# A planned Nyström attention and SiLU layer: q, k, landmarks and exp(C) of the later batches turned by DMA, scores over 64 rows

## The chip, the cores and the metric

The kernel runs on one core of a Trainium2 chip. TensorE (PE) multiplies into PSUM, VectorE (DVE) and ScalarE (ACT) read PSUM and write SBUF, GpSimd (POOL) works on SBUF alone, and SyncE (SP) issues DMAs. POOL issues DMAs too. Each engine runs its own instructions in order and waits on semaphores for the others. The metric is the time of one execution in microseconds (us).

## What is computed

For 8 batches of 8 heads, with a sequence of 576 and a head of 64, the reference computes attention with 32 landmarks, which are means over 18 neighbouring rows, and then a layer with SiLU:

```python
q_lm = q.reshape(B, H, m, S // m, D).mean(axis=3)
k_lm = k.reshape(B, H, m, S // m, D).mean(axis=3)
A = sm(q, k_lm)
Bm = sm(q_lm, k_lm)
C = sm(q_lm, k)
Z = Bm.transpose(0, 1, 3, 2) / (norm1(Bm) * norminf(Bm) + 1e-06)
for _ in range(6):
    Z = 2 * Z - Z @ Bm @ Z
attn = A @ Z @ C @ v
h = x @ w_in                       # x: attn with the heads side by side
out = (h * (1.0 / (1.0 + np.exp(-h)))) @ w_out
```

`sm` is a softmax over products scaled by 1/8. All inputs and the output are float32; the kernel works in bfloat16 with float32 sums.

## The kernel before

**One batch.** The 8 heads of a batch are held as two groups (`qd`) of four. The rows of q and k (`qn`, `kn`) come from HBM with 128 pairs of head and landmark on the partitions and 18 rows of 64 in each. `landmarks` sums the 18 rows: on TensorE for batches 0 to 2, on POOL from batch 3 on (`tree`, then `lm`). `turn` (lines 459 and 466) and the end of `landmarks` (line 446) turn q, k and the landmarks on VectorE. Its turn works in blocks of 32 by 32 words of 32 bits, so that the 64 numbers of a head end up as 32 partitions with pairs side by side. A score over 64 numbers is therefore two products over 32 rows (`o` = 0 and 1), the second added to the first: `scores_b` for Bm, `scores_a_of` for A and `scores_c` for C. From batch 2 on, those of Bm and A are one block of 48 products.

After the scores, VectorE takes maxima (`cmax`, `bmax`, `amax`), ScalarE takes exponentials (`exps_c` writes `pc`, which is exp(C), `exps_a` writes `ea`), and `values` turns `pc` with 12 products by an identity matrix on TensorE into PSUM, copies the result to `pt` (line 711; on VectorE from batch 2 on) and multiplies it with v (`vn`): C v. `norm_b` and `steps_x` are a serial chain of small products on TensorE and copies on VectorE that gives Z C v, and `z_of` brings it into the form `zt`. `weights_a` normalizes `ea` and turns it into `at`.

**The two layers.** `mix` multiplies `zt` with `w_in` into `m`, in products of 64 rows by 512 columns (64*32). `layer1` multiplies `m` with `at` (rows `h<-at,m`), and ScalarE writes SiLU of it to `g`. `layer2` multiplies `g` with `w_out` (rows `o<-w_out_sb,g`, 512 columns, 16 products for a tile of 128 rows of the output), ScalarE copies it to one of four buffers `ost`, and SP stores it, 64 rows a DMA.

**Buffers.** `qT` and `kT` exist once; `qn`, `kn`, `vn`, `lm` and `lmT` twice, in turn. A load of q or k for batch b + 2 goes into the buffer that batch b's turns read. PSUM is held as two double banks `h`, two banks `o` and two banks `t`.

**The order.** Every operation is recorded in `_Plan` with an engine, a cost and a priority, with the buffers that it reads and writes. `SEQ` is the order in which the steps are recorded (E: one batch's attention, M: its mix, L: its layer 1 or a part of it), `SHIFT` changes single priorities, `XM` is a margin behind which `layer1`'s products are taken as ready. `schedule` gives each operation a start and puts each engine's instructions out in that order. The costs only choose the order: what runs on the chip is that order, with semaphores where the data demands them. Nearly all products are issued in one helper, line 243, and are told apart by their tiles.

Of the kernel before, what the change touches and what calls it, by code (L numbers as in the profile page):

```python
# [8 lines left out]
BF = mybir.dt.bfloat16  # L9
# [7 lines left out]
SEQ = ['E0', 'M0', 'S1', 'L0', 'X1', 'K2', 'M1', 'E2', 'L1', 'E3', 'M2', 'L2.0.4', 'L2.4.16', 'M3', 'E4', 'L3', 'M4', 'E5', 'L4', 'E6', 'M5', 'L5', 'E7', 'M6', 'L6', 'M7', 'L7']  # L17
# [3 lines left out]
SHIFT = {'DVE gx t 3': 2.5, 'DVE qT qn 3': -0.25, 'POOL ea arec 1': 1, 'DVE lmT lm 3': 3.0, 'PE t gx 3': 2, 'DVE crec csum 3': -0.25, 'DVE asum ea 0': -0.5, 'POOL kn 1': -0.5, 'DVE at ea 3': 2, 'DVE asum ea 2': 2.5, 'ACT ea s 3': 1.0, 'PE t qn 0': -1, 'DVE bs t 3': -0.5, 'POOL qn 3': -1, 'DVE m h 0': -1.75, 'POOL kn 3': -1.0, 'DVE qT qn 1': 1, 'POOL bmd bm 0': -0.25, 'POOL kn 2': -2.5, 'DVE pt h 1': 2, 'PE t gx 2': -1, 'PE t xp 0': -0.25, 'PE t lmT 1': 0, 'ACT ea s 1': 1, 'ACT xp h 0': -2, 'PE t bt 1': 2, 'DVE m o 0': 2, 'ACT lm h 2': 0.5, 'DVE bm t 3': 0.25, 'DVE m h 1': 1, 'PE t gc1g 0': 0.5, 'DVE cmax h 2': 0.25, 'PE h m 0': -2, 'DVE mask 0': 0.5, 'DVE bsum t 1': -0.25, 'PE o g 0': 0.5, 'DVE at ea 2': 0.5, 'PE o g 2': 2, 'DVE kT kn 0': -1, 'POOL bmd bm 2': -1, 'PE t lmT 2': 0.5, 'DVE n t 1': -2, 'PE t kn 0': 1, 'DVE at ea 0': 1, 'POOL vn 1': 2, 'PE h m 2': -0.25, 'PE o lmT 0': 1, 'PE h pt 1': -0.25, 'DVE rn n 2': 3, 'PE o g 1': 2, 'DVE gc0t t 1': 0.5, 'PE t lmT 3': -0.5, 'PE t bt 0': 0.25, 'ACT ost3b o 3': 0.25, 'PE h zt 0': 1, 'DVE lmT lm 2': -2, 'PE h zt 1': 1, 'DVE n t 2': 1, 'POOL qn 1': -0.5, 'DVE brec bsum 3': 0.5, 'DVE bt gc0t 1': 2, 'DVE brec bsum 1': 0.25, 'DVE cneg cmax 3': 1, 'ACT t bs 2': -1, 'DVE bmax t 2': -0.25, 'POOL bmd bm 3': -0.25, 'DVE gc0g t 1': -0.25, 'POOL ea arec 2': 2, 'POOL tree kn 3': 2, 'DVE lmT lm 1': -0.5, 'POOL qn 0': -0.25, 'DVE gc1g t 1': 0.25, 'DVE bs t 2': 0.5, 'DVE bsum t 3': 0.5, 'DVE n t 5': -0.25, 'PE t qn 1': 0.5, 'DVE bm t 7': -1, 'PE h pc 0': -0.25, 'PE t kn 1': -0.5, 'DVE s h 6': -2, 'DVE bmax t 7': -0.5, 'ACT pc h 6': 0.5, 'PE h lmT 3': -1, 'PE t bm 3': 0.25, 'DVE rn n 1': 0.25, 'DVE bt bm 2': 0.25, 'DVE amax s 7': -0.5, 'ACT pc h 1': -0.5, 'POOL qn 4': -0.5, 'DVE pt h 2': 0.25, 'DVE kT kn 2': -0.5, 'DVE pt h 4': 0.25, 'DVE n t 3': 1, 'DVE bmd t 0': -2, 'DVE bs t 1': 1, 'ACT m h 5': 1, 'DVE bmax t 1': -2, 'ACT ost o 7': 1, 'DVE crn crec 0': -0.5, 'PE t gc0t 1': 0.5, 'PE t xp 2': -1, 'PE t gx 5': 2, 'DVE gx t 2': 1, 'DVE kT kn 3': 0.25, 'PE o g 3': 2, 'DVE pt h 7': -1, 'DVE crec csum 7': -1, 'PE h zt 3': -1}  # L21
# [4 lines left out]
FLAGS = {'st0': 'DDDAAA', 'st1': 'DAAADD', 'pt0': 'SS', 'pt1': 'SA', 'sub0': 'DP', 'sub1': 'PD', 'mul0': 'PP', 'mul1': 'PP', 'lm1': 'EE', 'lm2': 'EE', 'lz': 1}  # L26
# [4 lines left out]
XM = 0.12  # L31
# [181 lines left out]
def kernel(  # L213
# [25 lines left out]
    def sb(name, shape, dt):  # L239
        return pool.tile(shape, dt, tag=name, name=name)  # L240
# [17 lines left out]
    lm = [sb(f"lm{i}", [128, 2, 2, D], BF) for i in range(2)]  # L258
    lmT = [sb(f"lmT{i}", [128, 2, 2, LM, 2], BF) for i in range(2)]
# [5 lines left out]
    pc = sb("pc", [128, 2, 6, 96], BF)  # L265
# [52 lines left out]
    def emit_consts():  # L318
        V.memset(tiny, 0.0)
        V.memset(zero, 0.0)  # L320
        V.memset(mask, 0.0)
        V.memset(nmask, 0.0)
        V.memset(eps, 0.0)
        for a in range(4):
            V.memset(mask[32 * a:32 * a + 32, a, :], 1.0)
            V.memset(nmask[32 * a:32 * a + 32, a, :], -1.0)
            V.memset(eps[32 * a:32 * a + 1, :], 1e-6)
        V.memset(xp, 0.0)
        V.memset(heads_ps, 0.0)
        for a in range(4):  # L330
            V.memset(heads_ps[32 * a:32 * a + 32, a:a + 1], 1.0)
# [10 lines left out]
    def constants():  # L342
        P.add("DVE", 1.5, emit_consts, w=["mask", "xp", "zero", "tiny", "t0"], prio=-10)
# [29 lines left out]
    def load(t, src, b):  # L373
        if t == "v":
            def f():
                for t3 in range(3):
                    G.dma_start(  # L377
                        out=nat[t][b % 2][32 * t3:32 * t3 + 32].rearrange(
                            "p h j d -> p h (j d)"),
                        in_=src[b].rearrange("h (l t j) d -> t l h (j d)",  # L380
                                             t=3, j=6)[t3])
            P.add("POOL", 2.0, f, w=[f"{t}n{b % 2}"], dma=[0.95] * 3,
                  prio=-5 if b == 0 else -0.5)
            return
# [7 lines left out]
        P.add("POOL", 1.4, f, w=[f"{t}n{b % 2}"],  # L392
              dma=[1.4, 1.4], prio=-5 if b == 0 else -0.5)
# [4 lines left out]
    def landmarks(b):  # L398
        p2 = b % 2
        for ti, t in ((1, "k"), (0, "q")):  # L400
# [30 lines left out]
            else:  # L431
                tr, tk = tree, "tree"

                def add(o, a, c, n, r, w):
# [7 lines left out]
                add(lm[p2][:, ti], tr[:, :, 0], tr[:, :, 8], 128, [tk],  # L442
                    [f"lm{p2}.{ti}"])

# [9 lines left out]

    def turn(b):
        p2 = b % 2
        for qd in range(2):
            def f(qd=qd):
                V.transpose(  # L459
                    out=kT[:, qd].bitcast(FP).rearrange("p c t l o -> p t c (l o)"),  # L460
                    in_=nat["k"][p2][:, qd].bitcast(FP).rearrange(
                        "p (t c) w -> p t c w", c=6))
            dve(576, f, r=[f"kn{p2}"], w=[f"kT.{qd}"], prio=3 if b else 0.2)
        for qd in range(2):
            def f(qd=qd):
                V.transpose(  # L466
                    out=qT[:, qd].bitcast(FP).rearrange("p i l o -> p (i l o)"),
                    in_=nat["q"][p2][:, qd].bitcast(FP).rearrange(
                        "p i w -> p (i w)"))
            dve(576, f, r=[f"qn{p2}"], w=[f"qT.{qd}"], prio=3 if b else 0.9)  # L470
# [4 lines left out]
    def scores_b(b):  # L475
        lmr = lmT[b % 2]

        def f():
# [8 lines left out]
        if b < 2:  # L487
            pe(0.1, f, r=[f"lmT{b % 2}"], w=["t0", "t1"], mode="32",
               prio=1.2 if b == 1 else 0.1, margin=0.2, ni=32)
        else:  # L490
            def both():
                f()
                for hf in range(2):
                    scores_a_of(b, hf)
            pe(0.6, both, r=[f"lmT{b % 2}", "qT.0", "qT.1"],
               w=["t0", "t1", "h0", "h1"], mode="32", prio=0.1, margin=0.2, ni=96)
# [16 lines left out]
    def scores_c(b):  # L513


        lmr = lmT[b % 2]
        def f():
# [9 lines left out]
        pe(0.53, f, r=[f"lmT{b % 2}", "kT.0", "kT.1"], w=["h0", "h1"], mode="32",  # L527
           prio=0.1, margin=0.2, ni=64)
# [22 lines left out]

    def scores_a(b):

        for hf, (i0, i1) in enumerate(HALF):
# [9 lines left out]
            if b > 1:  # L564
                dve(2 * n, lambda i0=i0, i1=i1, n=n, hf=hf: V.transpose(  # L565
                    out=s_sb[:, i0:i1].rearrange("p i a m -> p a i m"),
                    in_=h_ps[hf][:, :, 0:n].rearrange("p a (i m) -> p a i m", m=LM)), r=ks, w=[f"s{hf}"], prio=0.2)
# [29 lines left out]
    def exps_c(b):  # L597
# [12 lines left out]
        for qd in range(2):  # L610
            act(576, lambda qd=qd: A.activation(  # L611
                out=pc[:, qd].rearrange("p (j c) n -> p j (c n)", j=2),
                in_=h_ps[qd][:, :, 0:SH], func=AF.Exp, bias=cneg[:, qd:qd + 1],
# [4 lines left out]
    def exps_a(b):  # L618
        gate = gates(b)
        for hf, (i0, i1) in enumerate(HALF):  # L620
            n = 64 * (i1 - i0)
            act(1.3 * n, lambda i0=i0, i1=i1: A.activation(  # L622
                out=ea[:, i0 // 2:i1 // 2].rearrange("p i a m j -> p i j (a m)"),
                in_=s_sb[:, i0:i1].rearrange("p (i j) a m -> p i j (a m)", j=2),
                func=AF.Exp, scale=sc / SEG),
# [68 lines left out]

    def values(b):


        for qd in range(2):
            def f(qd=qd):
                for j in range(6):  # L700
                    mm(h_ps[qd][0:96, j // 4, 128 * (j % 4):128 * (j % 4) + 128],
                       pc[:, qd, j], ident)
# [24 lines left out]
        def f():  # L727
            for qd in range(2):
                for j in range(6):
                    for h in range(4):  # L730
# [227 lines left out]
    def layer2(pr, ti):  # L958
# [8 lines left out]
        for c0 in range(0, DM, n):  # L967
# [16 lines left out]
            for x in bs_:  # L984
# [17 lines left out]
                else:  # L1002
                    P.add("SP", 0.7, lambda store=store, i0=i0, i1=i1: store(
# [111 lines left out]
```

## Time and profile before

| | |
|---|---|
| times of three runs | 271.65, 272.19, 272.21 us; median 272.19 |
| profiled execution | 271.19 us, of which 269.5 are its span |
| TensorE's clock granted, mean | 0.973 |
| DMA | 28.24 MB, 105 GB/s on the mean |
| layer 2's products, 128x512 | 556 records, 135.9 us busy |
| layer 1's products, 128x288 and others | 512 records, 76.4 us busy |

Busy times of products overlap, because they are pipelined: 373 ns is the mean of one `o` record, while 20 of them take 4.33 us in the chain, 0.217 each. Where a duration on the path is wanted, it is read from the start of one piece to the start of the next. Start-up takes the first 25 us or so. In it TensorE's clock is granted in part, and the loads fill the DMA engines. From 240 us on only layer 2 is left. The 40 slices of the page, 6.74 us each, show both ends:

```
PE   5678889998899999999999999999999999999993
DVE  3696866859967993389637973997278623000000
PEclk9965899999999999999999999999999999999999
DMA  6999999999395298324941370130303111103334
```

### The profile page before, as it was taken

To read this page: it belongs to the slowest core of one execution; us is meant where nothing else is said; L and a number is where in the kernel's file an instruction comes from. 1 tells how busy PE (TensorE), PEld (TensorE's weight loads), DVE (VectorE), ACT (ScalarE), POOL (GpSimd) and SP (SyncE) were. 2 spreads that over 40 slices of the span, in tenths; PEclk is the share of its full clock that TensorE was granted. 3 is DMA by queue.
4 is the path that set the end of the run, shared out by engine and by line. 5 is a ranking of instruction groups with operands and counts; after the bars stand their busy time and mean duration, and the time that the engine had idled before them with its cause. 6 is when DMAs were issued, how large, how long until landed. Compare 5 with 4: busy or idle time off the path is not lost.

```text
span 269.5 us, 6932 instructions
## 1 busy us (share of the span) xinstructions
PE 248.3 (92%) x2847; PEld 143.5 (53%) x2883; DVE 157.7 (59%) x384; ACT 162.0 (60%) x276; POOL 131.0 (49%) x158
## 2 busy tenths in 40 slices
PE   5678889998899999999999999999999999999993
PEld 3443545643574467446754566446744674664453
DVE  3696866859967993389637973997278623000000
ACT  2173369734874778658863887477827886861111
POOL 8546535799999998698429760330031300000000
PEclk9965899999999999999999999999999999999999
DMA  6999999999395298324941370130303111103334
GB/s 95 202 210 210 207 208 207 209 221 217 53 192 104 53 153 149 69 63 79 187 96 41 79 128 0 41 82 14 66 2 78 43 40 40 31 10 77 72 71 94
DMA packets 20832, 28.24 MB, mean 105 GB/s; under 512 B 2240, under 2 KB 11712, under 8 KB 20800
## 3 DMA queue, kind: packets, MB, share of 16 engines
q0 software_dynamic: 14880, 18.35, 40.9%
q1 hardware_dynamic: 5840, 9.38, 14.8%
q8 instruction: 22, 0.36, 0.5%
q10 hardware_dynamic: 80, 0.07, 0.1%
q14 instruction: 10, 0.08, 0.1%
HBM read 36.70 MB, written 9.44 MB: 171 GB/s over the span
## 4 chain that ended last, share of the span: by engine, by line
PE 79%; DVE 7%; DMA 6%; issue 3%; POOL 2%; ACT 2%; ACTq 0%; DVEq 0%; POOLq 0%
PE o L243 44%; PE h L243 30%; PE t L243 5%; DMA qn<-in_q_dram 4%; DMA vn<-in_v_dram 2%; DVE qT L466 1%; DVE cmax L530 1%; DVE m L871 1%; ACT ea L622 1%; DVE s_sb L565 1%; DVE asum L891 1%; DVE amax L581 0%; POOL s_sb L587 0%; ACT pc L611 0%; DVE pt L711 0%
## 5 line engine op out<-in xcount | busy, mean ns | idle before, releaser
L243 PE MATMUL o<-w_out_sb,g 128*128 128x512 bf16 (+1 forms) x556 | 135.9, 373 | 3.4 <-issue 2.4
L243 PEld LDWEIGHTS <-g 128*128 128x128 bf16 x592 | 53.8, 98 | 51.1 <-issue 7.9
L243 PE MATMUL h<-at,m 128*128 128x288 bf16 (+2 forms) x512 | 76.4, 288 | 2.7 <-DVE m L871 1.1
L951 ACT ACTIVATE g<-h 128x576 bf16<-128x576 f32 x112 | 67.6, 651 | 17.5 <-PE h L243 17.4
L243 PEld LDWEIGHTS <-m 128*128 128x128 bf16 x512 | 49.7, 99 | 28.6 <-issue 2.9
L982 ACT COPY ost<-o 128x512 f32<-128x512 f32 (+1 forms) x37 | 21.2, 574 | 39.1 <-PE o L243 38.9
L587 POOL TENSOR_TENSOR s_sb<-s_sb,amax 128x640 f32<-128x640 f32 (+1 forms) x14 | 16.0, 1156 | 31.2 <-DVE amax L581 30.0
L803 DVE SCALAR_TENSOR_TENSOR gx<-gx,t 128x384 bf16<-128x384 bf16 x30 | 16.4, 547 | 17.8 <-PE t L243 17.7
L436 POOL TENSOR_TENSOR tree<-tree 128x512 f32<-128x512 f32 (+2 forms) x30 | 24.6, 820 | 1.7
L832 DVE CAST m<-h 128x1024 bf16<-128x1024 f32 x14 | 17.0, 1215 | 14.3 <-PE h L243 14.3
L900 POOL TENSOR_TENSOR ea<-ea,arec 128x512 bf16<-128x512 bf16 (+1 forms) x16 | 18.4, 1161 | 11.0 <-DVE arec L895 7.3
L835 ACT CAST m<-h 128x1024 bf16<-128x1024 f32 x14 | 14.2, 1013 | 12.5 <-PE h L243 11.8
L622 ACT ACTIVATE ea<-s_sb 128x512 bf16<-128x512 f32 (+1 forms) x16 | 13.3, 848 | 8.0 <-POOL s_sb L587 7.7
L377 POOL DMA_DIRECT2D vn<-in_v_dram x24 | 14.1, 594 | 6.7 <-DMA w_out_sb<-in_moe_w_out_dram 1.9
L436 POOL TENSOR_TENSOR tree<-kn 128x1152 f32<-128x1152 bf16 x5 | 11.8, 2369 | 10.2 <-DMA kn<-in_k_dram 10.1
L611 ACT ACTIVATE pc<-h,cneg 128x576 bf16<-128x576 f32 x16 | 11.6, 731 | 4.2 <-DVE cneg L533 4.0
L934 ACT ACTIVATE g<-h 128x512 bf16<-128x512 f32 (+1 forms) x16 | 9.6, 648 | 6.8 <-PE h L243 6.8
L466 DVE STREAM_TRANSPOSE qT<-qn 128x576 f32<-128x576 f32 x16 | 11.9, 763 | 2.8 <-DMA qn<-in_q_dram 2.8
L459 DVE STREAM_TRANSPOSE kT<-kn 128x576 f32<-128x576 f32 x16 | 11.7, 747 | 2.4 <-DMA kn<-in_k_dram 2.4
L891 DVE TENSOR_REDUCE asum<-ea 128x16 f32<-128x512 bf16 (+1 forms) x16 | 11.6, 732 | 1.7 <-ACT ea L622 1.7
L530 DVE TENSOR_REDUCE cmax<-h 128x1 f32<-128x576 f32 x16 | 11.5, 752 | 1.3 <-PE h L243 0.8
L436 POOL TENSOR_TENSOR tree<-qn 128x1152 f32<-128x1152 bf16 x5 | 11.8, 2369 | 0.4
(116 smaller groups left out, 281.2 us busy)
## 6 DMA issues: line engine op xcount, KB each, us to landing
out_dram<-ost SPq DMA_DIRECT2D x70, 128.0 KB, 2.4
kn<-in_k_dram POOLq DMA_DIRECT2D x16, 288.0 KB, 8.5
qn<-in_q_dram POOLq DMA_DIRECT2D x16, 288.0 KB, 7.7
vn<-in_v_dram POOLq DMA_DIRECT2D x24, 192.0 KB, 6.5
w_out_sb<-in_moe_w_out_dram POOLq DMA_DIRECT2D x4, 512.0 KB, 16.1
w_in_sb<-in_moe_w_in_dram POOLq DMA_DIRECT2D x4, 256.0 KB, 10.1
w_in_sb<-in_moe_w_in_dram POOLq DMA_DIRECT2D x2, 512.0 KB, 13.2
out_dram<-ost SPq DMA_DIRECT2D x3, 64.0 KB, 2.1
```

The costliest lines, as they stand in the source:

```text
L243: nc.tensor.matmul(out=out_ap, lhsT=lhsT, rhs=rhs, start=start, stop=stop, tile_position=tp, skip_group_check=True)
L436: lambda: G.tensor_tensor(out=o, in0=a, in1=c, op=OP.add),
L466: V.transpose(out=qT[:, qd].bitcast(FP).rearrange("p i l o -> p (i l o)"), in_=nat["q"][p2][:, qd].bitcast(FP).rearrange("p i w -> p (i w)"))
L587: E.tensor_tensor(out=sv, in0=sv, in1=mv.unsqueeze(2).to_broadcast((128, 2 * (i1 - i0), LM)), op=OP.subtract),
L622: act(1.3 * n, lambda i0=i0, i1=i1: A.activation(out=ea[:, i0 // 2:i1 // 2].rearrange("p i a m j -> p i j (a m)"), in_=s_sb[:, i0:i1].rear ...
L803: dve(2 * (192 - lo), lambda a=a, lo=lo, dst=dst: V.scalar_tensor_tensor(out=dst, in0=gx[a][:, :, lo:192], scalar=2.0, in1=t_ps[0][:, 0:38 ...
L832: dve(1024, lambda: V.tensor_copy(out=dst, in_=h_ps[1]), r=["h1"], w=[f"m{b % 2}.{ci}"], prio=0.1)
L835: act(1024, lambda: A.copy(out=dst, in_=h_ps[0]), r=["h0"], w=[f"m{b % 2}.{ci}"], prio=-1)
L891: dve(n, lambda ev=ev, p0=p0, p1=p1: V.tensor_reduce(out=asum[:, p0:p1].rearrange("p i a j -> p (i a) j"), in_=ev.rearrange("p n m j -> p ...
L900: lambda ev=ev, p0=p0, p1=p1, E=V if on_dve else G: E.tensor_tensor(out=ev, in0=ev, in1=arec[:, p0:p1].rearrange("p i a j -> p (i a) j").u ...
L951: act(576, lambda dc=dc, hp=hp: A.activation(out=g[:, dc, c0:c0 + S].rearrange("p (a n) -> p a n", a=2), in_=hp[:, :, 0:SH], func=AF.Silu) ...
L982: act(n, lambda ob=ob, c0=c0: A.copy(out=os_[:, c0:c0 + n], in_=ob[:, 0:n]), r=[ok], w=[sk] if c0 == 0 else [sk + "b"], prio=0.5)
```

## The change

Six things change.

- From batch 4 on (`TB`), `turn` and the end of `landmarks` issue transposing DMAs from SP in place of VectorE's turns. A DMA turns whole blocks of 128 by 128, so that the 64 numbers of a head lie on 64 partitions. POOL writes the landmarks twice side by side (`lmd`, 256 columns), so that both halves of the partitions get them.
- With that, scores are single products over 64 rows (`fd`, `scores_ad`): 8 for Bm in place of 16, 32 of half the columns for A in place of 32, 16 for C in place of 32.
- From batch 5 on (`PB`), `values` turns `pc` with two transposing DMAs a batch from SP into `pt`, in place of 12 products and two copies. For that `pc` is 128 wide, cleared once at the start, and 96 of each 128 are written, in all batches.
- From batch 4 on, q and k are loaded with one DMA each in place of two, and the rows of v are read in another order in C v.
- The loads of q and k of batch 7 are recorded as due after C v of batch 5. In the built program this is a place in POOL's queue, not a semaphore.
- `SEQ` moves `E3` behind `L2.0.4`, `XM` goes from 0.12 to 0.24, some twenty entries of `SHIFT` are new or changed, both halves of `pt` of batch 1 are copied whole on ScalarE, and the cost of a store on SP follows its number of DMAs.

In the built order SP's queue then holds 18 transposing DMAs among the stores: 4 of landmarks (128x4x128), 8 of q and k (128x18x128) and 6 of `pc` (128x6x128).

```diff
-SEQ = ['E0', 'M0', 'S1', 'L0', 'X1', 'K2', 'M1', 'E2', 'L1', 'E3', 'M2', 'L2.0.4', 'L2.4.16', 'M3', ...
+SEQ = ['E0', 'M0', 'S1', 'L0', 'X1', 'K2', 'M1', 'E2', 'L1', 'M2', 'L2.0.4', 'E3', 'L2.4.16', 'M3', ...
-FLAGS = {'st0': 'DDDAAA', 'st1': 'DAAADD', 'pt0': 'SS', 'pt1': 'SA', ..., 'lz': 1}
+FLAGS = {'st0': 'DDDAAA', 'st1': 'DAAADD', 'pt0': 'SS', 'pt1': 'AA', ..., 'lz': 1, 'tb': 4, 'pb': 5}
+TB, PB = FLAGS['tb'], FLAGS['pb']
-XM = 0.12
+XM = 0.24
...
+    lmd = [sb(f"lmd{i}", [128, 2, 2, 2, D], BF) for i in range(2)]
+    lmdT = [sb(f"lmdT{i}", [128, 2, 2, 128], BF) for i in range(2)]
-    pc = sb("pc", [128, 2, 6, 96], BF)
+    pc = sb("pc", [128, 2, 6, 128], BF)
...
+        V.memset(pc, 0.0)
...
+        gate = [cv[b - 2]] if b >= PB + 2 and b - 2 in cv else []
         def f():
+            if b >= TB:
+                G.dma_start(out=dst, in_=rows.rearrange("(c p) n -> p c n", p=128))
+                return
...
+                add(lmd[p2][:, ti],
+                    tr[:, :, 0].unsqueeze(2).to_broadcast((128, 2, 2, D)),
+                    tr[:, :, 8].unsqueeze(2).to_broadcast((128, 2, 2, D)), 256, [tk],
                     [f"lm{p2}.{ti}"])
+        if b >= TB:
+            P.add("SP", 1.25, lambda: nc.sync.dma_start_transpose(
+                out=lmdT[p2].rearrange("p t a n -> p (t a) n"),
+                in_=lmd[p2].rearrange("p t a u d -> p (t a u d)")),
+                r=[f"lm{p2}.0", f"lm{p2}.1"], w=[f"lmT{p2}"], prio=-2, lat=2.8)
+            return
...
+        if b >= TB:
+            for t, dst in (("k", kTd), ("q", qTd)):
+                P.add("SP", 2.3, lambda t=t, dst=dst: nc.sync.dma_start_transpose(
+                    out=dst.rearrange("p a i n -> p (a i) n"),
+                    in_=nat[t][p2].rearrange("p a i d -> p (a i d)")),
+                    r=[f"{t}n{p2}"], w=[f"{t}T.0", f"{t}T.1"], prio=-1, lat=4.7)
+            return
...
+        def fd():
+            for qd in range(2):
+                for h in range(4):
+                    for par in range(2):
+                        r0, c0 = 64 * par, 32 * h
+                        mm(h_ps[qd][c0:c0 + 32, par, 0:SH],
+                           lmdT[b % 2][r0:r0 + 64, 0, qd, c0:c0 + 32],
+                           kTd[r0:r0 + 64, qd, :, c0:c0 + 32].rearrange(
+                               "p (t c) l -> p c t l", t=3), tp=(r0, c0))
...
+    def scores_ad(b, hf):
+        p0, p1 = HALF[hf][0] // 2, HALF[hf][1] // 2
+        for qd in range(2):
+            for h in range(4):
+                for par in range(2):
+                    r0, c0 = 64 * par, 32 * h
+                    mm(h_ps[hf][c0:c0 + 32, par, 0:64 * (p1 - p0)].rearrange(
+                        "p (i a l) -> p i a l", a=2, l=LM)[:, :, qd],
+                       lmdT[b % 2][r0:r0 + 64, 1, qd, c0:c0 + 32],
+                       qTd[r0:r0 + 64, qd, p0:p1, c0:c0 + 32], tp=(r0, c0))
...
         for qd in range(2):
+            if b >= PB:
+                P.add("SP", 1.25, lambda qd=qd: nc.sync.dma_start_transpose(
+                    out=pt[:, qd], in_=pc[:, qd].rearrange("p j n -> p (j n)")),
+                    r=[f"pc{qd}"], w=[f"pt{qd}.0", f"pt{qd}.1"], prio=-3, lat=2.3)
+                continue
...
-                           vn[0:96, 4 * qd + h, j],
+                           vn[0:96, 4 * qd + h, j if b < TB else 2 * (j % 3) + j // 3],
...
+        cv[b] = P.nodes[-1]
```

More of the change, by code (lines that the diff above doesn't have):

```diff
@@ L342, in constants @@
     def constants():
-        P.add("DVE", 1.5, emit_consts, w=["mask", "xp", "zero", "tiny", "t0"], prio=-10)
+        P.add("DVE", 1.5, emit_consts, w=["mask", "xp", "zero", "tiny", "t0", "pc0", "pc1"], prio=-10)
         P.add("POOL", 0.5, emit_ident, w=["s0"], prio=-5)
@@ L391, in f @@
             G.dma_start(out=dst[64:128], in_=blk[:, 1:3])
-        P.add("POOL", 1.4, f, w=[f"{t}n{b % 2}"],
-              dma=[1.4, 1.4], prio=-5 if b == 0 else -0.5)
+        P.add("POOL", 0.75 if b >= TB else 1.4, f, w=[f"{t}n{b % 2}"],
+              dma=[2.8] if b >= TB else [1.4, 1.4], after=gate, prio=-5 if b == 0 else -0.5)
     HALF = ((0, 8), (8, SEG))
@@ L491, in both @@
             def both():
-                f()
+                (fd if b >= TB else f)()
                 for hf in range(2):
-                    scores_a_of(b, hf)
-            pe(0.6, both, r=[f"lmT{b % 2}", "qT.0", "qT.1"],
-               w=["t0", "t1", "h0", "h1"], mode="32", prio=0.1, margin=0.2, ni=96)
+                    (scores_ad if b >= TB else scores_a_of)(b, hf)
+            pe(0.35 if b >= TB else 0.6, both, r=[f"lmT{b % 2}", "qT.0", "qT.1"],
+               w=["t0", "t1", "h0", "h1"], mode="64" if b >= TB else "32", prio=0.1,
+               margin=0.2, ni=80 if b >= TB else 96)
         pr = (-1, 1.5, 0.1)[min(b, 2)]
@@ L550, in scores_a_of @@
                        start=(o == 0), stop=(o == 1), tp=(r0, c0))
+    def scores_ad(b, hf):
+        p0, p1 = HALF[hf][0] // 2, HALF[hf][1] // 2
+        for qd in range(2):
+            for h in range(4):
+                for par in range(2):
[4 more added lines that the diff above has]
+                       qTd[r0:r0 + 64, qd, p0:p1, c0:c0 + 32], tp=(r0, c0))
     def scores_a(b):
@@ L701, in f @@
                     mm(h_ps[qd][0:96, j // 4, 128 * (j % 4):128 * (j % 4) + 128],
-                       pc[:, qd, j], ident)
+                       pc[:, qd, j, 0:96], ident)
             pe(0.36, f, r=[f"pc{qd}", "ident"], w=[f"h{qd}"], mode="full", prio=0.1,
@@ L1002, in layer2 @@
                 else:
-                    P.add("SP", 0.7, lambda store=store, i0=i0, i1=i1: store(
+                    P.add("SP", 0.64 * (i1 - i0), lambda store=store, i0=i0, i1=i1: store(
                         nc.sync, i0, i1), r=rk, w=[], lat=2.5)
```

54 lines of the change are left out of this document (40 added, 14 removed).

## The prediction

> **What bounds the kernel now.** I read the page's busy times and chain first, then TensorE's waits, then busy times by stretch, and last the chain piece by piece through one batch. Per batch I call "scores" the products with the landmarks, C v the product of the turned exp(C) with v, `m` products layer 1 (rows h<-at,m) and `o` products layer 2 (rows o<-w_out_sb,g).
>
> ```profile
> PE 248.3 (92%) x2847; PEld 143.5 (53%) x2883; DVE 157.7 (59%) x384; ACT 162.0 (60%) x276; POOL 131.0 (49%) x158
> ...
> PE 79%; DVE 7%; DMA 6%; issue 3%; POOL 2%; ACT 2%; ACTq 0%; DVEq 0%; POOLq 0%
> ```
>
> TensorE (PE) is 92% busy and 79% of the chain that ended last. Its waits from 82 us to the end, and two stretches (length, then busy time of PE, PEld, DVE, ACT, POOL with instruction counts, granted clock, DMA share, GB/s):
>
> ```profile
> PE o L243 <- issue: 2.1, 13, 0.2
> PE h L243 <- ACT g L951: 0.4, 1, 0.4
> ```
> ```profile
> 52.00:82.00 30.00, 27.42 (x357) 15.51 (x360) 21.50 (x50) 17.93 (x31) 29.00 (x33) 1.00 0.93 176
> 167.00:195.00 28.00, 27.52 (x322) 16.21 (x325) 19.84 (x45) 19.64 (x32) 5.29 (x5) 1.00 0.22 49
> ```
>
> The reader is to see two regimes. From 82 us TensorE waits 2.5 us in all, 2.1 of it short "issue" pauses, at full clock, because `o` products of earlier batches fill whatever gap a batch's serial work leaves. There a microsecond less of TensorE work is a microsecond less of time, and a faster VectorE is worth nothing. From 52 to 82 us it is idle for 2.6 us, waiting for ScalarE and VectorE: there the order decides. The chain through batch 6 (start, length, what):
>
> ```profile
> 168.15 0.17 PE t L243 x16
> 168.31 0.52 PE h L243 x30
> 168.84 0.16 issue
> 168.99 1.67 PE o L243 x7
> 170.67 0.63 PE h L243 x31
> ...
> 175.29 0.34 PE h L243 x6
> ...
> 176.23 0.34 PE h L243 x6
> ...
> 177.86 0.56 PE h L243 x16
> 178.41 0.53 PE t L243 x48
> ```
>
> These are the scores of B and A (48 small products, 0.84 us from 168.15 to 168.99), those of C (0.63 us), the two groups that turn exp(C) (0.34 each), half a mix (16 products of 64 rows by 512 columns, 0.56) and C v (48 products, 0.53, thus 11 ns each).
>
> **The change, part by part.**
>
> *Scores over 64 rows (batches 4 to 7).* B and A go from 48 products to 8 + 32 = 40, C from 32 to 16. A product over 64 rows needs no second half to be added. The nearest row for C is the half mix, the same 64*32 form: 16 products in 0.56 us at 512 columns, so 0.56 x 288/512 = 0.32 at 288; I take 0.37 for the change of form around it. That is 0.63 - 0.37 = 0.26 saved. B and A: 40 products at the 11 ns of C v are 0.44, with the 0.16 pause 0.60, so 0.24 saved. (0.26 + 0.24) x 4 = 2.0 us. Ends: 0.8 us, if B and A gain only their share of products (0.84 x 8/48 = 0.14) and C costs the whole 0.56 (0.07 saved); 2.6 us, if C costs 0.32 (0.31 saved) and B and A, bound by columns streamed, save 0.34.
>
> *exp(C) turned by DMA (batches 5 to 7).* Twelve products a batch go: 2 x 0.34 x 3 = 2.04 us. They stood in TensorE's queue, with `o` products ready behind, so all of it comes off the path.
>
> *VectorE.* It loses 16 turns of q and k (rows of 763 and 747 ns, 12.1 us), 4 of the landmarks (301 ns) and 6 copies of exp(C) (943 ns, 5.7 us). On the path: nothing, for `o` products hide that work now. If that cover were gone at C v, a copy and its wait would be a gain of 1 us a batch; I count none. The extra clearing of `pc` at the start (three times the 0.27 us of `zero`) falls into the 1.21 us in which VectorE waits there for `ident`.
>
> *POOL.* Loads of q and k become one DMA instead of two (eight issues of 0.6 us less), the doubled landmarks cost 0.73 instead of 0.46 (128x256 against 128x128) eight times. POOL is off the path after 160 us. The loads of batch 7 move behind the ea products of batch 5. In the built order no semaphore holds them to C v, so only their place in POOL's queue does: about 159 us, against 124 to 131 now. Landing (8.5), two sums of 5.6 (2.37 + 1.28 + 0.73 + 0.46 + 0.73) and the landmark transfer (2.4) end near 181, and the scores of batch 7 come near 196: 15 us of cover. Behind them in POOL's queue are v and the sums of batch 7 alone.
>
> *SP's queue: 18 transposing DMAs among the stores.* The trace has no such DMA. The nearest rows:
>
> ```profile
> out_dram<-ost SPq DMA_DIRECT2D x70, 128.0 KB, 2.4
> kn<-in_k_dram POOLq DMA_DIRECT2D x16, 288.0 KB, 8.5
> ...
> vn<-in_v_dram POOLq DMA_DIRECT2D x24, 192.0 KB, 6.5
> ```
>
> q and k are 576 KB each: 10.8 us at the store's pace, 17 at the load's. They may start when the scores of the batch before have read `qT` and `kT`, and are needed a stage later, 28 us (196.31 for batch 7 less 168.15 for batch 6). Either pace is covered if the two overlap; one after the other, 34 us are not (a rival below). Behind a waiting transfer stand only stores; four `ost` buffers let three more `o` blocks go on, and the store lands in 2.4.
>
> exp(C) is 192 KB a half, and here the cover is short. I add up the products between the scores of C and C v in the built order (`o` 0.215, four `m` 0.49, half a mix 0.56): batch 5: 32 `o`, 12 `m` and 0.2 of small ones, 8.5 us; batch 6: 36 `o`, two half mixes and 0.2, 9.0; batch 7: 30 `o`, two half mixes and 0.2, 7.7. ScalarE ends the second exp(C) 3.3, 3.9 and 4.2 us after the scores of C now (by the timeline 150.7, 175.2 and 204.1 against 147.4, 171.3 and 199.9). So the second transfer has 5.2, 5.1 and 3.5 us. At 2.4 us, the store, C v never waits; at 6.5, v's load, it waits 1.3 + 1.4 + 3.0 = 5.7 us. I take the store's pace by size, 2.4 x 1.5 = 3.6: same queue, no HBM end, and DMA engines a quarter busy there (share 0.22) where v's load runs beside q and k (0.7 to 1.1). That is 0.1 us, and 0.3 with the issue in front of it.
>
> The Trainium skill, page Advanced Engine Details and Errata, X-Bar Transpose (TRN2), says that such transfers are as fast as plain ones; by it the wait would be 0. No run here shows it yet.
>
> *New plan.* Batch 3's scores move behind mix 2 and a quarter of layer 1 of batch 2, and the margin `XM` doubles, which only reorders. In the first regime this acts: in batch 2 both turning groups now stand ahead of the norm's product, so that it and what follows waits for the later exp(C). The named waits from 52 to 82 us are 2.1 us. All gone would be -2; doubled, +2. The order puts more serial work of batch 1 and 2 side by side with fewer `o` between, so I take +1.0.
>
> *Sum.* -2.0 - 2.04 + 0.3 + 1.0 = -2.7 us. The profiled execution took 271.19 us (span 269.5, and 1.7 around it), so 268.5; it lies 1.0 below the median of the runs shown, 272.19, so the median comes to 269.5.
>
> **Rivals.**
>
> *C v waits for its transfers (slower).* If a transposed half lands like v's load, the three C v wait 5.7 us: -4.04 + 5.7 + 1.0 = +2.7, 274.9. It decides from a landing of some 5.5 us: then the waits (0.3 + 0.4 + 2.0, and 1.0 of plan) have eaten most of the gain. For it: a transpose writes in small pieces, and no row shows one. Against: DMA is quiet there.
>
> *Transposes go block by block.* At v's pace, 34 us a batch for q and k, 13 for exp(C), one after the other: C v would wait (13 - 4.6) x 3 = 25 us, and the median come to 294. The Trainium skill, page VectorE: DVE Perf Modes, The three transpose paths, gives 1309 ns for a 128x128 block by DMA against 390 by TensorE; by it, an estimate, the twelve blocks of exp(C) would take 15.7 us. No row bears it out.
>
> *The plan gives the gain back.* If the first regime loses 3 to 4 us, the time is 272 give or take 0.5. Against: only 2.6 us are idle there now.
>
> *The order gains too.* The 2.1 us of waits go: 266.5.
>
> **How the numbers follow.** Forecast 0.53 (its own range 268.0 to 271.2: the ends of the scores, and 0 to 2 of plan), C v waits 0.24, block by block 0.05, given back 0.13, gains too 0.05. The range 267.6 to 274.9 leaves out the blocks, half of the gains and the worse part of the waits. This measurement can tell about 0.2% (0.54 us) from no change: faster 0.60, same 0.10, slower 0.30.
>
> **What would show it.** Scores of C near 0.37 us and of B and A near 0.60; no h<-ident,pc from batch 5 on; from 82 us still under 4 us of TensorE waits; transposes of exp(C) landing in under 4 us. It is wrong if TensorE waits for `pt` before C v, if SP's stores hold up `ost`, or if the stretch from 45 to 82 us is longer by over 2 us.

## The result, and the profile after

The changed kernel takes 278.50 us (median of 4 runs, 277.89 to 279.54) against 271.94 for the kernel before, run beside it (271.65 to 272.21): a ratio of 1.0245, 95% interval 1.0211 to 1.0279. It is slower by 6.6 us, where 2.7 us less were forecast, and it lies outside the range. The profiled execution took 277.89 us, 276.2 of it span. In what follows a ratio under 1 is faster than the kernel before; where a kernel's times fall into two groups (f4 and h3 below), the ratio compares the lower group, so the times stand beside it.

From the page of the changed kernel, the busy times and the chain by engine:

```profile
PE 248.1 (90%) x2715; PEld 142.4 (52%) x2751; DVE 143.5 (52%) x359; ACT 163.2 (59%) x275; POOL 128.8 (47%) x150
...
PE 52%; DMA 26%; POOL 7%; DVE 6%; issue 4%; ACT 2%; ACTq 0%; POOLq 0%; DVEq 0%
```

TensorE's share of the chain fell from 79 to 52%, and DMA's rose from 6 to 26%. TensorE's waits of the changed kernel from 82 us to the end (in total, times, longest), where the kernel before showed 2.5 us in all:

```profile
PE h L244 <- ACT g L1039: 7.7, 1, 7.7
PE o L244 <- issue: 1.6, 10, 0.2
PE t L244 <- DMA pt<-pc: 0.9, 2, 0.5
```

One pause of 7.7 us is there, and little else. Milestones place the loss. From the timelines, the start of the first half mix of batches 3 and 4, and the end of the span (e1 and g2 are experiments below):

| us | before | changed | e1 | g2 |
|---|---|---|---|---|
| start to mix of batch 3 | 110.4 | 112.1 | 113.6 | 113.5 |
| mix of batch 3 to mix of batch 4 | 28.7 | 37.1 | 27.4 | 27.4 |
| mix of batch 4 to the end | 130.4 | 127.0 | 127.2 | 127.1 |

The work between the milestones is nearly equal: counted by their weight loads, 150, 72 and 370 products of layer 2 fall into the three rows of the kernel before, and 156, 68 and 368 into those of the three others; one takes 0.22 us. The last row is the gain of batches 5 to 7, 3.2 to 3.4 us, of which two products fewer are 0.4. The middle row holds the loss. The chain of waits of the changed kernel through it (start, length, what):

```profile
96.88 14.45 DMA kT<-kn
111.33 0.29 issue
111.61 8.02 DMA kn<-in_k_dram
...
119.78 2.37 POOL tree L444
...
130.71 1.01 POOL s_sb L661
...
133.91 1.28 ACT L1039
...
135.20 0.66 ACT g L1039
135.86 0.04 issue
135.90 1.12 PE h L244 x4
```

It reads from the top. The transposing transfer of k of batch 4 lands after 14.45 us. Only then may the load of k of batch 6 (k6) overwrite the buffer `kn` that it read. The load lands 8.0 us later, POOL sums k6 and q6 (nine additions, the first into `lmd` among them, to 130.7), and only behind them does POOL start the subtraction `s_sb<-s_sb,amax` of batch 4, for which ScalarE and then TensorE wait. POOL's own rows of the same stretch (start, length, operation, count, idle time before it and its releaser):

```profile
111.61 0.76 POOL L395 DMA_DIRECT2D kn<-in_k_dram  x1 [7.06 <-DMA kT<-kn]
119.78 2.36 POOL L444 TENSOR_TENSOR tree<-kn 128x1152 f32<-128x1152 bf16 x1 [7.41 <-DMA kn<-in_k_dram]
130.67 2.27 POOL L661 TENSOR_TENSOR s_sb<-s_sb,amax 128x512 f32<-128x512 f32 x2
```

POOL sat idle for 14.5 us with the head of its queue waiting, and the subtraction carries no wait of its own: it stood in line. Then the clock. The same stretch of the kernel before and of the changed one (length, then busy PE, PEld, DVE, ACT, POOL with counts, granted clock, DMA share, GB/s):

```profile
110.00:139.00 29.00, 28.42 (x324) 16.27 (x326) 20.00 (x45) 19.94 (x32) 19.80 (x22) 1.00 0.58 108
```
```profile
110.00:139.00 29.00, 20.95 (x235) 10.40 (x238) 14.56 (x35) 13.23 (x20) 18.60 (x19) 0.89 0.71 135
```

After the pause the granted clock is 0.50 from 135.8 to 138 us and 0.60 from 138 to 140, before it is 1.00 again, and eight products of layer 1 take 2.08 us where they take 1.14 in g2. So 37.1 - 27.4 = 9.7 us are the pause, 7.7, and 2.0 of slower products behind it; the clock alone gives 2.2 x 0.5 + 2.0 x 0.4 = 1.9, an estimate.

### The profile page after: what moved, and what is told of

It is laid out like the page before. It is cut to its first block, busy times and chain, and to the rows that moved or that the text cites. A ratio compares the mean times of both kernels' runs of the same rounds, so it can differ in the third digit from the quotient of the medians.

```text
span 276.2 us, 6675 instructions
## 1 busy us (share of the span) xinstructions
PE 248.1 (90%) x2715; PEld 142.4 (52%) x2751; DVE 143.5 (52%) x359; ACT 163.2 (59%) x275; POOL 128.8 (47%) x150
## 3 DMA queue, kind: packets, MB, share of 16 engines
q0 software_dynamic: 14752, 18.35, 40.7%
## 4 chain that ended last, share of the span: by engine, by line
PE 52%; DMA 26%; POOL 7%; DVE 6%; issue 4%; ACT 2%; ACTq 0%; POOLq 0%; DVEq 0%
PE o L244 29%; PE h L244 20%; DMA kn<-in_k_dram 7%; DMA qn<-in_q_dram 6%; DMA w_out_sb<-in_moe_w_out_dram 6%; DMA kT<-kn 5%; POOL tree L444 5%; PE t L244 3%; DMA pt<-pc 2%; DVE cmax L585 1%; DVE amax L655 1%; DVE pt L798 1%; ACT ea L703 1%; DVE s_sb L638 1%; DVE qT L497 1%
## 5 line engine op out<-in xcount | busy, mean ns | idle before, releaser
L244 PE MATMUL h<-at,m 128*128 128x288 bf16 (+2 forms) x512 | 78.3, 289 | 11.4 <-ACT g L1039 8.3
L244 PEld LDWEIGHTS <-g 128*128 128x128 bf16 x592 | 54.4, 98 | 52.6 <-issue 7.9
L923 ACT CAST m<-h 128x1024 bf16<-128x1024 f32 x14 | 14.2, 1012 | 10.9 <-PE h L244 10.7
L444 POOL TENSOR_TENSOR tree<-kn 128x1152 f32<-128x1152 bf16 x5 | 11.8, 2368 | 11.6 <-DMA kn<-in_k_dram 11.5
L685 ACT ACTIVATE pc<-h,cneg 128x576 bf16<-128x576 f32 x16 | 11.8, 738 | 4.1 <-DVE cneg L588 3.9
L444 POOL TENSOR_TENSOR tree<-qn 128x1152 f32<-128x1152 bf16 x5 | 11.8, 2367 | 0.4
L244 PE MATMUL t<-gx 128*128 128x192 bf16 (+1 forms) x72 | 11.4, 241 | 0.0
L655 DVE TENSOR_REDUCE amax<-s_sb 128x16 f32<-128x512 f32 (+1 forms) x16 | 11.3, 731 | 0.1
```

Of the source, the lines that this page charges most:

```text
L244: nc.tensor.matmul(out=out_ap, lhsT=lhsT, rhs=rhs, start=start, stop=stop, tile_position=tp, skip_group_check=True)
L444: lambda: G.tensor_tensor(out=o, in0=a, in1=c, op=OP.add),
L655: dve(2 * n, lambda sv=sv, mv=mv: V.tensor_reduce(out=mv, in_=sv, axis=AX.X, op=OP.max), r=[f"s{hf}"], w=[f"amax{hf}"], prio=0.5 if b > 1 ...
L923: act(1024, lambda: A.copy(out=dst, in_=h_ps[0]), r=["h0"], w=[f"m{b % 2}.{ci}"], prio=-1)
```

## The experiments

In all of them the plan's finished order is edited: `find(kind, n)` gives operations recorded with batch n (`POOL kn 4` is the load of k6, `POOL qn 4` of q6, `POOL vn 3` of v5), and `behind(a, x)` moves them to stand after x. Everything else is the changed kernel. The diffs are abridged; names such as `sums_of_batch_6` stand for the operations that they name.

**e1: loads behind.**

```diff
+    behind(find("POOL qn", 4) + find("POOL vn", 3), find("POOL kn", 4)[0])
```

> The changed kernel, with one move in POOL's queue: the loads of q of batch 6 and v of batch 5 stand behind the load of k of batch 6, so that no load is in flight while k of batch 4 is turned. Theory: that transfer took 14.45 us because it ran beside those loads; then it lands in 5 to 6 us like the other three, the load of k 6 and its sums come 8 us earlier, the subtraction of batch 4's maxima is in time, and the pause of 7.7 us on TensorE and the slow clock behind it go: 268 to 270 us. Rival 1: the transfer is slow of itself (the first of its kind, or the stores): it still takes 12 to 15 us and the time stays at 277 to 281. Rival 2: the pause comes from ScalarE or TensorE's order: the transfer gets short and the time stays.

Measured: 270.24 us, ratio 0.9925 (0.9890 to 0.9961), faster than the kernel before by under 1%. The rows of the transfer and of the subtraction:

```profile
98.56 2.69 SPq L483 DMA_TRANSPOSE kT<-kn  x1
```
```profile
122.02 2.27 POOL L661 TENSOR_TENSOR s_sb<-s_sb,amax 128x512 f32<-128x512 f32 x2
```

The transfer of k of batch 4 lands after 6.3 us in place of 14.4, k6 is issued at 105.43 and the subtraction starts at 122.02. No pause is left. The loads of q6 and v5 beside the transfer are thus a cause.

**e2, e3: sums behind the subtraction, with the loads unmoved and moved.**

```diff
+    behind(sums_of_batch_6, find("POOL s amax", 4)[-1])
```

> The changed kernel, with one move in POOL's queue: the sums of batch 6's landmarks stand behind the subtraction of batch 4's maxima; the loads and transfers stay where they are. Theory (POOL's in-order queue carries the late landing to batch 4): the transfer of k of batch 4 stays at 12 to 15 us, yet the pause goes, 268 to 270 us. Rival 1 (transfer slow of itself) says the same of the time here. Rival 2 (the pause comes from ScalarE or TensorE's order) expects 277 to 279.

> The changed kernel with both moves. Theory: one of the two was enough, so the same as the better of them within 0.5 us, 268 to 270 us, with no wait of TensorE over 1 us behind 82 us.

Measured: e2 279.19 (ratio 1.0280, 1.0238 to 1.0323), e3 278.14 (1.0234, 1.0181 to 1.0288). Both missed, by 9 and 8 us, and in e3 the transfer of k was quick (5.7 us at most). POOL's rows of e3 tell why:

```profile
121.38 2.26 POOL L661 TENSOR_TENSOR s_sb<-s_sb,amax 128x512 f32<-128x512 f32 x2 [13.44 <-DVE amax L655]
123.62 2.36 POOL L444 TENSOR_TENSOR tree<-kn 128x1152 f32<-128x1152 bf16 x1
...
135.35 0.67 POOL L769 TENSOR_TENSOR bmd<-bm,mask 128x256 bf16<-128x256 bf16 x1
...
137.73 2.27 POOL L988 TENSOR_TENSOR ea<-ea,arec 128x512 bf16<-128x512 bf16 x2
```

The subtraction now starts when its maximum is there, but 10.9 us of sums went between it and `bmd` and `ea`, which TensorE needs as well; it waits 6.4 us for `gx` in e3 and 7.7 in e2. The expectation had followed one operation of batch 4 and not the two behind it in the same queue.

**f1: sums behind all of batch 4's work.**

```diff
+    behind(sums_of_batch_6, find("POOL ea arec", 4)[-1])
```

> The changed kernel with one move in POOL's queue: the sums of batch 6 (k and q, ten additions, 10.9 us) go behind the last product ea<-ea,arec of batch 4, thus behind all that TensorE waits for there (subtraction s_sb, bmd, ea); the loads of q6 and v5 stay where they are. Theory A (the pause comes from what stands ahead of batch 4's work in POOL's queue; moving the sums only past the subtraction missed because bmd and ea still stood behind them, at 135.35 and 137.73): the transposing transfer of k of batch 4 stays late (14 us and more to landing), yet the subtraction starts when its maximum is there, near 120.5, ea ends near 125, TensorE's pause near 130 falls below 1 us, time 268.5 to 271. Theory B (the slow transfer itself holds TensorE, or the late landmarks of batch 6 cost the same later): 274 or more.

Measured: 270.10 (0.9939, 0.9913 to 0.9965). The subtraction starts at 121.95, released by its maximum, `bmd` at 124.99, and no pause is left. In its profile the transfer landed after 8.2 us, not 14, so this profile doesn't show a late one without harm.

And the move has a fault that its expectation overlooked. It takes POOL's sums of batch 6 along, but not the transfer that turns the landmarks that they write. That one keeps its place on SP's queue, now ahead of the sums:

```profile
126.35 1.27 SPq L460 DMA_TRANSPOSE lmdT<-lmd  x1
```
```profile
138.33 0.73 POOL L444 TENSOR_TENSOR lmd<-tree 128x256 bf16<-128x256 f32 x1
```

So it turns what batch 4 left in the buffer, and f1 leaves out the landmarks of batch 6. In a whole kernel this transfer would wait at the head of SP's queue until POOL's second sum is done, near 145, and the stores behind it with it. The 270.10 us are therefore not the time of a kernel that computes the reference, and f1 shows the mechanism only up to 126 us. The same holds for g1 and h3 below (landmarks turned at 127.02 and 142.04, written from 139.02 and 148.11 on), and for no other run.

**f3, f4: which load.** Only q6, or only v5, goes behind k6.

> The changed kernel with the load of q of batch 6 alone moved behind the load of k of batch 6 in POOL's queue; the three loads of v of batch 5 stay ahead of it. Theory A1 (any load beside the transposing transfer of k of batch 4 slows it, in proportion to its bytes): its landing near 9 to 10 us, half way between 5.4 and 14.5, the pause of TensorE 0 to 2 us, time 270 to 272.5. Theory A2 (the load of q, which is issued with the transfer, does it alone): landing 5 to 6, no pause, 268.5 to 271. Theory A3 (the loads of v do it): landing 13 or more, time as the changed kernel, 277 to 279.

> The changed kernel with the three loads of v of batch 5 alone moved behind the load of k of batch 6; the load of q of batch 6 stays ahead, beside the transposing transfer of k of batch 4. Theory A1: landing 9 to 10 us, 270 to 272.5. Theory A2 (q's load does it): landing 13 or more, 277 to 279. Theory A3 (v's loads do it): landing 5 to 6, 268.5 to 271.

Measured: f3 270.53 (0.9950, 0.9919 to 0.9982), the transfer landing after 4.7 us, as theory A2, by which q's load does it, had expected. f4: of its twelve times seven lie between 270.9 and 273.2 and five between 276.3 and 278.3 (ratio 1.0007, 0.9984 to 1.0031). The profile is one of the upper five. POOL's row and the row of the transfer on SP's queue in f4:

```profile
112.96 0.75 POOL L395 DMA_DIRECT2D kn<-in_k_dram  x1 [7.61 <-DMA kT<-kn]
```
```profile
99.09 5.49 SPq L483 DMA_TRANSPOSE kT<-kn  x1
```

So the load of q6, issued 0.1 us after the transfer, is enough in this execution (13.3 us to landing). The seven lower times suggest that it isn't in every one; none of them was profiled. That v's loads are harmless doesn't follow: in f3 they start at 102.05, when that transfer has 1.2 us left.

**g2: a second meeting**, in batch 5, where nothing waits for the transfer.

```diff
+    behind(find("SP kT kn", 5), find("SP lmT lm", 6)[0])
+    behind(find("POOL qn", 5), find("POOL bmd bm", 4)[0])
```

> The kernel with the loads of q6 and v5 moved behind the load of k6 (270.24 us, no late transfer), and one meeting more, in batch 5, where nothing needs the transfer for 15 us: the transposing transfer of k of batch 5 goes behind the landmarks' transfer of batch 6 in SP's queue (issued near 126 instead of 123), and the load of q7 goes behind batch 4's bmd in POOL's queue (issued near 126 as well), followed by the loads of v6 near 129. Theory A2 (a q load issued together with a transposing transfer, then v loads behind it, makes that transfer late, wherever it happens): k's transfer of batch 5 takes 8 us or more to landing instead of 5.4; time unchanged, 269 to 271.5, since the scores of C of batch 5 come near 148. Rival (something else of batch 4 makes it late, such as what SP or VectorE do there): 5 to 6 us to landing.

Measured: 268.95 (0.9893, 0.9839 to 0.9947). The row of the transfer of k of batch 5 and the landings of the transfers of k in 118 to 150 us:

```profile
125.87 7.47 SPq L483 DMA_TRANSPOSE kT<-kn  x1
```
```profile
DMA to landing us min/median/max: 5.4/10.3/15.1
```

15.1 us, and the issue itself holds SP for 7.5 in place of 2.7. So the meeting makes a transfer late in another batch too; the kernel is quick because nobody waits there.

**f5: the old plan with the new transfers; e4: the new plan alone.**

```diff
-SEQ = [..., 'L1', 'M2', 'L2.0.4', 'E3', 'L2.4.16', ...]    (f5, with SHIFT, XM, pt1)
+SEQ = [..., 'L1', 'E3', 'M2', 'L2.0.4', 'L2.4.16', ...]
-'tb': 4, 'pb': 5      (e4)
+'tb': 9, 'pb': 9
```

> The changed kernel with the sequence, the shifts, XM and pt1 of the kernel before; transposing transfers, scores over 64 rows and the gate stay. The prediction's terms without its plan: 271.66 - 2.0 (scores) - 2.04 (exp(C) no longer turned on TensorE) + 0.3 = 268. Theory A (the gains are there and the loss is one place of the new order): 267 to 269.5, no pause of TensorE over 2 us between 90 and 150. Rival (the transfers beside loads cost wherever they stand, so the old order loses as well): 273 or more, with a transfer of k or q that lands after more than 10 us ahead of a pause.

> The changed kernel without any transposing DMA: TB = PB = 9, so that all turns, scores and loads are those of before, with the new SEQ, SHIFT, XM and copies. Theory: the new plan by itself costs what batches 1 to 3 show (the second mix of batch 2 and all before it come 0.8 us later for equal work), so 272 to 273.5 us. Rival: the plan was the larger loss, 274 or more.

Measured: f5 270.33 (0.9960, 0.9945 to 0.9976), no transfer of k over 5.6 us; e4 277.05 (1.0166, 1.0110 to 1.0222). f5 has no pause over 1.4 us between 90 and 150, so the loss of the changed kernel needs the new plan's order, though f5 is 0.8 us above its expected range. e4 came out as its rival said, 274 or more. By the milestones it is 4.6 us later than the kernel before at the mix of batch 3, and its middle row is 2.2 longer. That doesn't make the plan the larger loss in the changed kernel: without the transfers the planner lays out another order, with its own late load (k6 9.1 us) ahead of batch 4's subtraction (127.14), and the same plan with the transfers takes 270.24 in e1, as long as the old one in f5.

**g1: both moves; g3: both, and exp(C) by DMA from batch 4 on.**

> Both moves that helped alone, together: the loads of q6 and v5 behind the load of k6, and the sums of batch 6 behind batch 4's last ea<-ea,arec. Theory A (each cures the same pause, one by making the load of k6 early, the other by letting batch 4's work past its sums): nothing is left to gain, time as with either alone, 269.5 to 270.8, kT of batch 4 landing in 5 to 6 us. Rival (each left a part of the loss, so they add up): below 269.

> Both moves, and exp(C) turned by DMA from batch 4 on instead of 5 (twelve products of TensorE less, 0.68 us; the gate on the loads then holds from batch 6 on, so the loads of k6, q6 and v5 come behind batch 4's ea). Theory A (from 82 us on TensorE's own work sets the time, so what is taken off it comes off the time): 0.7 us less than with both moves, near 269.4. Rival (the transfers of exp(C) land too late in batch 4, or the loads do, or the new order loses it): 270 or more, with a wait of TensorE for pt or for batch 6 above 1 us.

Measured: g1 269.67 (0.9922, 0.9894 to 0.9949), as with either move alone, but like f1 without batch 6's landmarks. g3 282.93 (1.0383, 1.0337 to 1.0428): 13 us more than e1 and g1. In its order batch 6's landmarks are turned behind their sums (152.26). TensorE's largest wait in g3, and the rows on SP's and POOL's queues before it:

```profile
PE t L244 <- DMA pt<-pc: 12.0, 2, 10.6
```
```profile
160.45 4.62 SPq L781 DMA_TRANSPOSE pt<-pc  x1
```
```profile
158.99 0.76 POOL L395 DMA_DIRECT2D kn<-in_k_dram  x1
159.75 0.72 POOL L395 DMA_DIRECT2D qn<-in_q_dram  x1
```

In g3 the loads of k7 and q7 meet the transfers of exp(C) of batch 5, which then land after up to 10.3 us, against 2.7 to 3.4 in the changed kernel. A third meeting, now with the rival that the prediction had named (C v waits). In the changed kernel k7 is issued at 165.30, when these transfers, issued from 161.91 on, have all but landed.

**h1, h2, h3: lateness without a meeting.** In e1's order the transfer of k of batch 4 is held in SP's queue behind two or three more output blocks; in h3 the sums stand last as well. In h2 and h3 the loads that follow it keep their places behind it, and in h2 the first sum too.

```diff
+    kt = find("SP kT kn", 4)
+    behind(kt, stores_after_it[1])      (h1;  [2] in h2 and h3)
```

> The kernel with the loads of q6 and v5 behind the load of k6 (270.24 us, transfer of k of batch 4 issued 98.56, landed 104.9, subtraction s_sb at 122.0, no pause), and that transfer held back in SP's queue behind two more output blocks, without any load beside it: issue near 103.9, landing near 109.3. Theory A (chain: transfer lands, load of k6 5 to 8 us, sums of batch 6 10.9 us, then the subtraction; TensorE pauses when that starts later than about 124.5, the start that made no pause with q's load alone moved): subtraction at 126 to 128.5, pause 1.5 to 4 us, time 272 to 275. Theory B (the lateness does harm only through the busy DMA engines of the meeting): no pause, 269.5 to 271.

> As the kernel before it, the transfer held back behind three more output blocks: issue near 112.7, landing near 118, still before the scores of C of batch 4 at 121. Theory A: subtraction at 135 to 137, pause 10.5 to 12.5 us and up to 2 us of lower clock behind it, time 281 to 285. Theory B: no pause over 2 us, 269.5 to 272.

> The same late transfer (landing near 118), with the sums of batch 6 behind the last ea<-ea,arec of batch 4. Theory A: the load of k6 is issued near 118.4, before the maximum is there, so the subtraction starts when that is, near 122, and TensorE has no pause: 269 to 271. Rival (the late landing holds TensorE by another way, such as batch 6's landmarks): 274 or more.

Measured: h1 270.65 (0.9950, 0.9917 to 0.9982), h2 288.61 (1.0625, 1.0564 to 1.0686). h3: eleven times from 270.5 to 277.8, median 274.57 (ratio 1.0001, 0.9965 to 1.0036); its profile is the slowest of them. The rows of h2, POOL's and TensorE's:

```profile
118.42 0.76 POOL L395 DMA_DIRECT2D kn<-in_k_dram  x1 [15.37 <-DMA kT<-kn]
...
139.63 2.27 POOL L661 TENSOR_TENSOR s_sb<-s_sb,amax 128x512 f32<-128x512 f32 x2
```
```profile
144.86 2.08 PE L244 MATMUL h<-at,m 128*128 128x288 bf16 x8 [16.89 <-ACT g L1039]
```

Here the transfer itself took 6.2 us and was only issued late, and the pause is the longest of all. The start of the subtraction, counted from the start of the scores of C of batch 4, sets it:

| us | scores of C | subtraction | between | pause |
|---|---|---|---|---|
| h1 | 121.61 | 124.59 | 2.98 | none |
| f3 | 121.11 | 124.47 | 3.36 | none |
| f4 | 121.69 | 130.47 | 8.78 | 5.43 |
| changed | 119.59 | 130.67 | 11.08 | 7.73 |
| h2 | 119.39 | 139.63 | 20.24 | 16.89 |

The pause is the difference less 3.35 us, in all five of these kernels, each of which computes the whole reference. h1's expectation missed by two steps: the transfer was issued at 102.69, not 103.9, and landed 4.8 us later, not 5.4, and so the subtraction came just in time. h2's pause was longer than expected, because the load of k6 now met the transfer of q of batch 5 (whose issue took 7.96 us): POOL had k6 at 128.75, 10.3 us after its issue, where h1 had it after 5.6. h3 is between theory and rival. Its transfer of k of batch 4 is as late as in h2 (k6 issued at 120.67), and yet TensorE has no pause from 118 to 142 us: with the sums out of the way the subtraction starts at 123.87. Up to there the order is sound, so this is the late landing without harm that f1 didn't show. Behind it POOL waits 8.8 us for the transfer of batch 6's landmarks, and batch 5 pauses for 2.8 us. That transfer stands in SP's queue behind those of q and k of batch 5, whose issues take 6.7 and 14.6 us, but POOL waits for it only because it stands ahead of the sums, where f1's does. What a whole kernel would do there, no run shows.

## Why the prediction was wrong

**The step that failed** is the covering of the transfers of q and k: "Either pace is covered if the two overlap", and "Behind a waiting transfer stand only stores". The bound on the pace held (14.45 us is under the 17 allowed). But the cover of 28 us was counted to the reader of the result, the scores of batch 5's stage. Nobody was asked who next writes the buffer that the transfer reads: the load of k6, whose wait is at the head of POOL's queue. And behind it the queue held sums of batch 6 ahead of work of batch 4. What cover there was, h1 shows: its k6, issued 121.61 - 108.01 = 13.6 us ahead of the scores of C, cost nothing. In the changed kernel that point is 119.59 - 13.6 = 106.0, 9.1 us after the transfer's issue, not 28. The transfer made k6 5.6 us later than that, k6 itself took 8.0 in place of 5.5, and 0.4 was to spare: 7.7. "POOL is off the path after 160 us" was read from the stage where it held and said nothing of 97 to 131.

**The price of it** was nowhere in the sum: 7.7 us of pause, 2.0 of slower clock. With these 9.7 taken off, 278.5 would be 268.8, an estimate, near the 269.5 forecast. Of the rivals, "C v waits" had the right family (a transfer that lands late beside other traffic) but the wrong transfer; 274.9 was also short of it.

**Scores over 64 rows: right for C, at the low end for B and A.** 0.37 us for C was forecast, 0.60 for B and A. The timeline of batch 5 of the changed kernel (start, length, operation):

```profile
153.52 0.21 PE L244 MATMUL t<-lmdT 64*32 64x32 bf16 x8
153.56 0.51 PE L244 MATMUL h<-qT,lmdT 64*32 64x128 bf16 x32
154.22 2.11 PE L244 MATMUL o<-w_out_sb,g 128*128 128x512 bf16 x9 [0.16 <-issue]
156.26 0.44 PE L244 MATMUL h<-kT,lmdT 64*32 64x288 bf16 x16
156.63 0.39 PE L244 MATMUL o<-w_out_sb,g 128*128 128x512 bf16 x1
```

C takes 156.63 - 156.26 = 0.37, B and A with the pause 154.22 - 153.52 = 0.70. That is 0.14 less than the 0.84 before, where 0.24 was forecast, so four batches gain 0.4 us less. The 0.16 in both figures isn't a pause: ten weight loads of `g` follow here for nine records of `o`, and eight for seven in the kernel before, so the record of one product is missing. In g2 all ten are there, no pause is, and B and A take 0.48.

**exp(C) by DMA: right.** The sum gave -2.04 - 1.5 (three batches of scores) + 0.3 = -3.24 for batches 5 to 7; from the mix of batch 4 to the end it is 3.2 to 3.4 us less in the changed kernel, e1 and g2, or 2.8 to 3.0 without the two products fewer. TensorE waits 0.9 us for `pt`, 0.3 having been forecast, and these rows of its view of DMA issues (count, median us to landing) give the landings:

```profile
pt<-pc SPq DMA_TRANSPOSE x6, 2.8
lmdT<-lmd SPq DMA_TRANSPOSE x4, 3.5
qT<-qn SPq DMA_TRANSPOSE x4, 5.6
kT<-kn SPq DMA_TRANSPOSE x4, 5.4
```

2.8 us for exp(C), between the store's 2.4 and the 3.6 taken. The wait is longer than forecast all the same because the issue comes late: in batch 5 ScalarE is done at 160.0, but k's transfer and two stores stand ahead in SP's queue, and the two transfers are issued from 161.91 on. "Block by block" was far off. (Its 34 us for q and k are k's pace, 8.5 us for 288 KB; v's, 6.5 for 192, gives 39.)

**VectorE: right.** Clearing `pc` takes 0.70 us, and the wait for `ident` behind it falls from 1.21 to 0.40.

**New plan: +1.0 forecast.** At the mix of batch 3 the changed kernel is 1.7 us later and e1 3.2, with six more products of layer 2 done in both (1.3 us): +0.4 and +1.9. Their order is the same up to 97 us, but not their clock in the first 45: 0.89 and 0.77, and 0.85 in the kernel before. g2, with 0.85 too, is 3.1 later. But f5, with the old sequence, is 3.4 later as well, so what of this is the plan's isn't settled. Without the pause the sum comes near: f3, h1, e1 and g2 are at -1.4, -1.4, -2.0 and -2.9 us by their ratios, and -2.7 was forecast.

**The Trainium skill**, page Advanced Engine Details and Errata, section X-Bar Transpose (TRN2), says that such transfers are as fast as plain ones. Alone they are here: 576 KB land in 4.6 to 6.5 us in the changed kernel but for the late one, a load of that size in 5.6 (k in e1). Beside loads neither keeps its pace: the transfer takes 13.3 to 17.7 us in e2, f4, g2 and the changed kernel, and the load beside it 8.4 to 14.9, about as long in f4 and the changed kernel but far less in g2.

e1 and g2, which compute all of it, beat both kernels: 270.24 and 268.95 us.

## What to carry to other kernels

For a transfer that becomes slower or later, ask two things: when its result is read, and when the buffer that it reads is written again. Then look at what stands behind that writer in its engine's queue, whichever batch it is for: an in-order queue turns a wait of a load for batch 6 into a wait of batch 4. And place loads and transposing transfers apart, or where nobody waits for the transfer. Whoever moves the operations that write a buffer in a recorded order has to move its reader behind them too, as f1, g1 and h3 did not.

## What the runs showed of the hardware

A transposing transfer that meets a load is late, and mostly the load is late too. One of 576 KB, issued within 0.7 us of a load of as many bytes, landed after 8.2 us (f1), 13.3 (f4), 14.4 (changed), 15.1 (g2), 17.7 (e2), 17.9 (h2) and 19.8 (h3), against 4.5 to 6.6 where no load was issued with it (the transfers of k that follow the late ones of h2 and h3, 11.8 and 20.2, apart). The load beside it landed after 9.7, 12.5, 14.9, 8.4, 13.8, 10.2 and 13.5 us, in the same order, against 5.6 (k) and 7.6 (q) in e1. The row of q6 in the changed kernel, from its DMA issues of 97 to 111.3 us:

```profile
qn<-in_q_dram POOLq DMA_DIRECT2D x1, 576.0 KB, 14.9
```

The issue of the transfer can hold SP's queue as well, for 5.5 (f4), 6.7 (h3), 7.5 (g2) and 8.0 us (h2) in place of 2.7. It need not: in the changed kernel and e2 it took 2.9 and 3.6 us. The packets, from the pages of the kernel before and the changed one:

```profile
q1 hardware_dynamic: 5840, 9.38, 14.8%
```
```profile
q0 software_dynamic: 14752, 18.35, 40.7%
q1 hardware_dynamic: 31504, 15.80, 29.3%
```

The queue of SP gained 25,664 packets and 6.42 MB, thus 250 bytes a packet, against 18.35 MB / 14752 = 1244 of the loads. The Trainium skill, page DMA: Bandwidth & Descriptors, section Queues, rings and completion order, says that each DMA engine takes turns between queues packet by packet. By that, an estimate, a queue of packets a fifth as large would move a sixth of the bytes. It fits a late transfer beside a quick load, as in g2; why the load is late too in the other meetings, it doesn't say, and no run here shows the turns themselves. Nor is it settled why the times of one program fall into two groups (f4).

The pause also costs afterwards: in the changed kernel 7.7 us without products were followed by some 4 us at a granted clock of 0.50 and 0.60, a loss of about 2 us. In h2, 16.9 us without products were followed by 0.50 (144.8 to 147 us) and 0.68 (to 149.5).
